# Stage two of a spectral block: the order of its sums, who negates and copies its output, and when the modulation columns are made

## The chip, the cores and the metric

One core of a Trainium2 chip. The metric is the device time of one execution in microseconds, the median of several runs. The profile is of one further execution, recorded by the hardware profiler.

## The reference

The block is a transformer layer with adaptive layer norms. `x` is 2048 x 512, all in float32:

```python
mod = (silu(c) @ w_mod).reshape(1, 6, 1, 512)
sa, ca, ga, sb, cb, gb = (mod[:, i] for i in range(6))
h = layernorm(x) * (1 + ca) + sa
y = irfft2(rfft2(h) * (w_r + 1j * w_i))     # over both axes, 2048 x 512
x = x + ga * y
h = layernorm(x) * (1 + cb) + sb
x = x + gb * (mish(h @ w1 + b1) @ w2)       # 512 -> 1376 -> 512
```

## The kernel before

The two-dimensional transform is done with matrix products. Stage one (to about 50 us) does the row transform of 512 and the first factor of the column transform, stage two (about 50 to 96 us) the second factor, the product with the spectral weights and the first factor back, stage three (about 96 to 142 us) the second factor back, the row transform back and `x + ga * y`. The rest is the MLP, in 8 blocks of 256 rows, in which TensorE works almost without a break.

The order of the work is written out by hand (`manual_schedule`), with no planner's costs or due times: the function's body is a list of calls, and the compute engines take their instructions in that order and wait where they have to. A load that waits for its buffer can be issued behind later ones: in the trace the last modulation load stands behind the first weight loads of stage three.

**Stage two** works on 17 groups of frequencies. Sixteen are ordinary (one of 3 and fifteen of 4 frequencies, 128 columns each), and the group of frequency zero has functions of its own (`z_in`, `z_mul`, `z_prod`, `z_back`, `z_out`). `seq` puts the zero group in position 4 of 0 to 16. For an ordinary group there are these steps:

- `p2_in`: TensorE transposes four tiles (L472), ACT copies them out of PSUM (L475), POOL adds the shift (`p2_shift`, L483).
- `p2_mul`: TensorE multiplies by a constant matrix (L492). The result lies in one of two banks "B" or in the bank `spare`, in turn.
- `p2_prod`: the complex product with the weights. ACT copies the two halves crosswise into `o` (L512, L513), POOL multiplies `o` by one part of the weights (L514), DVE multiplies the bank in place by the other (L515).
- `p2_add`: DVE adds both and writes the sum into `a_sb` (L521). This frees the bank of `p2_mul`.
- `p2_out` and `store_d`: TensorE multiplies by a constant matrix (L530) into one of two banks "D", and the result goes to `dd[0]` and `dd[1]`, 32 lanes each, as three planes: real part, imaginary part and the negated real part. ACT copies two planes for each of both halves (L387, 128x256), and the negated plane comes from POOL (L393, from the copy in SBUF), for the narrow groups from ACT (L391), and for the last group from DVE (L389, from PSUM).

The main loop runs over s = 1 to 19. Step s does the sum of position s, the product of position s + 1, the input of position s + 3 and the output of position s - 3. The first products are made ahead of it, in a loop over the first five inputs. Around these stand, by step:

- `mod_fetch` (SP's queue) and `mod_late` (DVE, L115): the modulation vectors `ga`, `sb`, `cb` and `gb`, 128 values at a time. Each of 16 columns is a load of 256 KB into one of four buffers and one DVE instruction that multiplies it by the spread-out silu(c) and sums it. `when` gives their steps, 3 to 18.
- `load_wq`: the weights of later groups (512 KB each, on ACT's queue, L558), into the place of the weights last used.
- `z_back` at step 5: the zero group's way back, with ACT and DVE copying from one bank and POOL writing zeros (L405 to L407, L453 to L456). Its target is `early[0]`, free after the first groups.
- `flat` and `spread`: the gate column goes out to DRAM and comes back spread over the partitions (ACT's queue); `mod_gate` (DVE, L552) then multiplies the constants `kiv` of the row transform back by `ga`.
- the loads of `kc` (two of 1 MB, ACT's queue, L604), the constants of stage three.

**Stage three** runs over 16 tiles: `p3_col(s)` (L675, L676: matmuls of `dd` with `kc`; ACT's copy L678), `p3_row(s - 1)` (L685: matmuls with `kiv`; DVE's L688 adds to `x`), statistics of the new `x` (`norm_sums`, DVE) and, every few tiles, `norm_scale` (ACT L127, L128 and four small DVE instructions). Beside them the MLP's weights are loaded on SP's queue (`load_w1`, `load_w2`) and split into two float32r parts (`split_w1`: ACT L629, POOL L630; `split_w2`, `sum_w2`: L726, L727, L723), and the first block's input is normalised and transposed. The second gate is spread there as well. The first tile needs every group's output in `dd[0]`.

## Time and profile before

| | before |
|---|---|
| median of 3 runs | 390.59 us (389.32 to 393.05) |
| profiled execution | 389.15 us |
| span in the profile (first to last instruction) | 387.1 us |
| granted TensorE clock | 0.998 |
| busy: PE, PE weight loads | 376.2 us (97%), 341.4 us (88%) |
| busy: DVE, ACT, POOL | 297.7 us (77%), 253.0 us (65%), 107.0 us (28%) |

The span leaves out 389.15 - 387.1 = 2.05 us around the first and the last instruction. PE is TensorE's matmuls, PEld its weight loads, DVE VectorE, ACT ScalarE, POOL GpSimd, SP the engine that only issues transfers here; ACTq and SPq are the queues of ACT and SP. L512 is line 512 of the kernel. Matmuls overlap and their ends are modelled, so a busy PE isn't always at its limit. In a timeline, brackets tell how long the engine was idle before an instruction and what ended that.

### The profile page before, as it was taken

To read this page: it belongs to the slowest core of one execution; us is meant where nothing else is said; L and a number is where in the kernel's file an instruction comes from. 1 tells how busy PE (TensorE), PEld (TensorE's weight loads), DVE (VectorE), ACT (ScalarE), POOL (GpSimd) and SP (SyncE) were. 2 spreads that over 40 slices of the span, in tenths; PEclk is the share of its full clock that TensorE was granted. 3 is DMA by queue.
4 is the path that set the end of the run, shared out by engine and by line. 5 is a ranking of instruction groups with operands and counts; after the bars stand their busy time and mean duration, and the time that the engine had idled before them with its cause. 6 is when DMAs were issued, how large, how long until landed. Compare 5 with 4: busy or idle time off the path is not lost.

```text
span 387.1 us, 7132 instructions
## 1 busy us (share of the span) xinstructions
PE 376.2 (97%) x2612; PEld 341.4 (88%) x2612; DVE 297.7 (77%) x674; ACT 253.0 (65%) x532; POOL 107.0 (28%) x149
## 2 busy tenths in 40 slices
PE   8999989897999999999999999999999999999996
PEld 8999857676999998999999998998999899899985
DVE  1898957788489989878757856965965885987994
ACT  1798787996459548965845755764674674594751
POOL 0587746899257713300000000000000010017000
PEclk9999999999999999999999999999999999999999
DMA  7999976898043411100100100100100200112011
GB/s 239 375 356 341 363 310 200 246 352 316 6 152 92 129 49 28 56 1 2 54 2 1 56 2 0 56 1 2 55 2 0 75 1 2 50 59 110 2 54 54
DMA packets 21747, 41.14 MB, mean 106 GB/s; under 512 B 4017, under 2 KB 7185, under 8 KB 21457
## 3 DMA queue, kind: packets, MB, share of 16 engines
q1 hardware_dynamic: 19552, 33.75, 25.3%
q10 hardware_dynamic: 2160, 6.95, 5.4%
q8 instruction: 20, 0.33, 0.4%
q14 instruction: 15, 0.11, 0.1%
HBM read 36.49 MB, written 4.20 MB: 105 GB/s over the span
## 4 chain that ended last, share of the span: by engine, by line
PE 80%; ACT 6%; issue 3%; POOL 3%; DVE 3%; DMA 3%; ACTq 0%; POOLq 0%; DVEq 0%
PE bank L817 24%; PE bank L764 20%; PE bank L766 10%; PE bank L208 4%; PE bank L253 3%; PE bank L809 2%; PE bank L685 2%; PE bank L830 2%; PE bank L654 2%; PE bank L675 2%; PE bank L676 2%; DMA wm<-in_w_mod_dram 1%; ACT buf L512 1%; DMA buf<-in_B_w_dram 1%; PE bank L264 1%
## 5 line engine op out<-in xcount | busy, mean ns | idle before, releaser
L774 ACT ACTIVATE buf<-bank,b1n 128x256 f32<-128x256 f32 (+1 forms) x88 | 40.8, 472 | 66.9 <-PE bank L766 66.5
L775 DVE TENSOR_TENSOR buf<-buf,bank 128x256 f32<-128x256 f32 (+1 forms) x88 | 35.4, 417 | 38.6 <-ACT buf L774 38.6
L746 POOL TENSOR_TENSOR buf<-buf,modr 128x512 f32<-128x512 f32 (+1 forms) x3 | 3.9, 1299 | 183.0 <-DVE al L727 148.3
L727 DVE TENSOR_TENSOR al<-buf,ah 128x512 fp32r<-128x512 f32 (+2 forms) x85 | 53.0, 647 | 0.9 <-ACT ah L726 0.9
L764 PE MATMUL bank<-h2e,w1h 128*128 128x512 f32 (+1 forms) x176 | 48.5, 397 | 0.0
L764 PE MATMUL bank<-h2o,w1h 128*128 128x512 f32 (+1 forms) x176 | 48.3, 396 | 0.0
L726 ACT CAST ah<-buf 128x512 fp32r<-128x512 f32 (+2 forms) x85 | 43.0, 549 | 1.4 <-DVE buf L791 1.1
L791 DVE TENSOR_TENSOR buf<-buf 128x128 f32<-128x128 f32 x148 | 40.8, 317 | 3.5 <-ACT buf L781 2.2
L781 ACT ACTIVATE buf<-buf 128x512 f32<-128x512 f32 (+1 forms) x48 | 28.6, 596 | 14.7 <-DVE buf L775 14.6
L817 PE MATMUL bank<-w2a,ah 128*128 128x256 f32 x161 | 34.9, 286 | 0.0
L764 PEld LDWEIGHTS bank<-h2e,w1h 128*128 128x128 f32 (+1 forms) x176 | 30.1, 187 | 4.5
L764 PEld LDWEIGHTS bank<-h2o,w1h 128*128 128x128 f32 (+1 forms) x176 | 30.1, 187 | 4.4
L817 PE MATMUL bank<-w2b,ah 128*128 128x256 f32 x147 | 31.8, 283 | 0.0
L766 PEld LDWEIGHTS bank<-h2e,w1l 128*128 128x128 f32 (+1 forms) x176 | 26.7, 185 | 4.2
L766 PEld LDWEIGHTS bank<-h2o,w1l 128*128 128x128 f32 (+1 forms) x176 | 26.7, 185 | 4.2
L766 PE MATMUL bank<-h2e,w1l 128*128 128x256 f32 (+1 forms) x176 | 27.8, 280 | 0.0
L766 PE MATMUL bank<-h2o,w1l 128*128 128x256 f32 (+1 forms) x176 | 27.8, 280 | 0.0
L817 PEld LDWEIGHTS bank<-w2a,ah 128*128 128x128 f32 x161 | 26.7, 191 | 0.0
L676 PE MATMUL bank<-kc,d 128*128 128x128 f32 x128 | 24.8, 276 | 0.7 <-POOL d L393 0.7
L675 PE MATMUL bank<-kc,d 128*128 128x128 f32 x128 | 24.9, 276 | 0.5 <-ACT d L387 0.5
L817 PEld LDWEIGHTS bank<-w2b,ah 128*128 128x128 f32 x147 | 24.6, 191 | 0.0
L122 DVE BATCH_NORM_STATS2 st<-x 128x6 f32<-128x512 f32 x32 | 22.0, 688 | 0.4
(219 smaller groups left out, 987.5 us busy)
## 6 DMA issues: line engine op xcount, KB each, us to landing
buf<-in_B_w_dram SPq DMA_DIRECT2D x20, 256.0 KB, 3.1
x<-in_A_x_dram SPq DMA_DIRECT2D x16, 256.0 KB, 4.8
xring<-in_x_t_dram SPq DMA_DIRECT2D x16, 256.0 KB, 4.7
wm<-in_w_mod_dram SPq DMA_DIRECT2D x16, 256.0 KB, 5.7
out_dram<-x SPq DMA_DIRECT2D x7, 512.0 KB, 2.6
mraw<-in_km_dram SPq DMA_DIRECT2D x16, 128.0 KB, 4.4
wqa<-in_w_q_dram SPq DMA_DIRECT2D x4, 512.0 KB, 7.1
wqb<-in_w_q_dram SPq DMA_DIRECT2D x4, 512.0 KB, 6.9
```

The source lines that it names most:

```text
L122: nc.vector.bn_stats(t, x[:, n, :])
L675: nc.tensor.matmul(o, dj[:, 0:128], kc[0][:, n, :], start=True, stop=False)
L676: nc.tensor.matmul(o, dj[:, 64:192], kc[1][:, n, :], start=False, stop=True)
L726: nc.scalar.copy(h, r)
L727: nc.vector.tensor_tensor(l, r, plain(h), op=ALU.subtract)
L764: nc.tensor.matmul(ps, w1h[:, k, fs], h[:, k], start=(k == 0), stop=False)
L766: nc.tensor.matmul(ps[:, 0:256], w1l[:, k, fs], h[:, k, 0], start=False, stop=(k == 3))
L774: nc.scalar.activation(o, ps[:, 256:], AF.Identity, bias=b1n[:rows, f:f + 1])
L775: nc.vector.tensor_tensor(o, o, ps[:, 0:256], op=ALU.add)
L781: nc.scalar.activation(o, o, AF.Mish)
L791: nc.vector.tensor_tensor(o, p, q, op=op)
L817: nc.tensor.matmul(o, a[p][:, e], w2[t][q][:, r], start=(own and half == 0 and t == 1 and i == 0), stop=(end and i == 2 and (n, half) != ( ...
```

## The change

- In the loop ahead of the main loop the sum of position 0 (`p2_add`) is written before the product of position 1 (`p2_prod`).
- `store_d` gets a kind. In an ordinary step ("busy") POOL negates the first half only and DVE the second, from PSUM. In steps without a modulation column, 9, 11 and 18, ("free") DVE copies the second half as well. The narrow groups ("all") and the last group ("last") are as before.
- The zeros for `z_back` are written at step 2, and its last ACT copy is moved ahead of DVE's copy.
- Modulation columns: 11 remain in stage two, at steps 3, 4, 5, 6, 8, 10, 12, 14, 15, 16 and 17. Five are made in stage three, two in its step 0 and one in each of steps 1 to 3; their loads go into the buffers "t", two from step 17 on, the others each after an earlier column.
- `load_wq` goes one step earlier, the second load of `kc` goes from step 13 to 12, `mod_gate` from step 15 to 13, and `plus_one` from stage two's step 16 to stage three's step 3.
- In stage three `flat` and `spread` of the second gate go from steps 2 and 4 to 5 and 7, and `norm_scale` of the first four tiles from steps 3 and 5 to 4 and 7.

```diff
-    def store_d(ps, q0, nq, other=None):
+    def store_d(ps, q0, nq, kind="all"):
...
             s = src[:, 32 * i:32 * i + 32]
-            nc.scalar.copy(dst[:, :, 0:2, q0:q0 + nq], s)
-            if other:
-                nc.vector.tensor_scalar(dst[:, :, 2, q0:q0 + nq], s[:, :, 0, :], -1.0, None, op0=ALU.mult)
-            elif nq < 4:
-                nc.scalar.mul(dst[:, :, 2, q0:q0 + nq], s[:, :, 0, :], -1.0)
+            to, minus = dst[:, :, 0:2, q0:q0 + nq], dst[:, :, 2, q0:q0 + nq]
+            if kind == "free" and i:
+                nc.vector.tensor_copy(to, s)
             else:
-                nc.gpsimd.tensor_scalar(dst[:, :, 2, q0:q0 + nq], dst[:, :, 0, q0:q0 + nq], -1.0, None, op0=ALU.mult)
+                nc.scalar.copy(to, s)
+            if kind == "all":
+                nc.scalar.mul(minus, s[:, :, 0, :], -1.0)
+            elif kind == "last" or i:
+                nc.vector.tensor_scalar(minus, s[:, :, 0, :], -1.0, None, op0=ALU.mult)
+            else:
+                nc.gpsimd.tensor_scalar(minus, dst[:, :, 0, q0:q0 + nq], -1.0, None, op0=ALU.mult)
...
+    def z_space():
+        return early[0][:, 0, 0:256], early[0][:, 0, 256:512]
...
         turned(t1, pc[:, 0:P])
-        nc.gpsimd.memset(t2[0:96, 0:P], 0.0)
         nc.scalar.copy(t2[0:32, 0:P], pc[0:32, P:2 * P])
+        nc.scalar.copy(t2[64:96, 0:1], pc[64:96, P:P + 1])
         nc.vector.tensor_copy(t2[32:64, 1:P], pc[32:64, 2 * P - 1:P:-1])
-        nc.scalar.copy(t2[64:96, 0:1], pc[64:96, P:P + 1])
...
-        store_d(pd, q0, nq, g == seq[-1])
+        store_d(pd, q0, nq, "all" if nq < 4 else "last" if g == seq[-1] else "free" if free else "busy")
...
-    when = (3, 4, 5, 6, 7, 8, 9, 10, 11, 12, 13, 14, 15, 16, 17, 18)
+    when = (3, 4, 5, 6, 8, 10, 12, 14, 15, 16, 17)
...
+    def mod_second(k):
+        w = buf("t")
+        nc.sync.dma_start(w, wm_d[5 - (k == 0), (k - 1) % 4])
+        return w
...
                 p2_mul(seq[i // 2 - 1])
-                p2_prod(seq[i // 2 - 1])
                 if i == 4:
                     p2_add(seq[0])
+                p2_prod(seq[i // 2 - 1])
...
-            if 3 <= s < len(seq) + 3 and seq[s - 3] and groups[seq[s - 3]][0] < 32:
-                load_wq(groups[seq[s - 3]][0] // 4 + 8)
+            if 2 <= s < len(seq) + 2 and seq[s - 2] and groups[seq[s - 2]][0] < 32:
+                load_wq(groups[seq[s - 2]][0] // 4 + 8)
...
+            if s == 2:
+                nc.gpsimd.memset(z_space()[1][0:96, 0:P], 0.0)
+            if s == len(seq):
+                second = [mod_second(k) for k in range(2)]
...
-                p2_out(seq[s - 3])
+                p2_out(seq[s - 3], s != 13 and not work_mod[s])
...
-            if s == 15:
+            if s == 13:
                 mod_gate()
-            if s == 16:
-                plus_one(cols[:, 1, 1, :], cols[:, 1, 1, :])
-            if s in (11, 13):
+            if s in (11, 12):
...
+        for k in ((0, 1), (2,), (3,), (4,))[s] if s < 4 else ():
+            mod_column(second[k], gcol[:, 1, k - 1:k] if k else cols[:, 1, 1, 3:4], 1.0, second[k], scp)
+            if k < 3:
+                second.append(mod_second(k + 2))
+        if s == 3:
+            plus_one(cols[:, 1, 1, :], cols[:, 1, 1, :])
-        if s == 2:
+        if s == 5:
             st["gb"] = flat("gb", gcol[:, 1])
-        if s == 4:
+        if s == 7:
             spread(gbr, st["gb"])
...
-        if s in (3, 5):
-            norm_scale(s - 3, s - 1)
+        if s in (4, 7):
+            norm_scale(*((0, 2) if s == 4 else (2, 4)))
```

More of the change, by code (lines that the diff above doesn't have):

```diff
@@ L450, in z_back @@
         nc.tensor.transpose(pc[0:96, P:2 * P], y[:, 160:256], ident)
-        t1, t2 = early[0][:, 0, 0:256], early[0][:, 0, 256:512]
+        t1, t2 = z_space()
         turned(t1, pc[:, 0:P])
-        nc.gpsimd.memset(t2[0:96, 0:P], 0.0)
         nc.scalar.copy(t2[0:32, 0:P], pc[0:32, P:2 * P])
+        nc.scalar.copy(t2[64:96, 0:1], pc[64:96, P:P + 1])
         nc.vector.tensor_copy(t2[32:64, 1:P], pc[32:64, 2 * P - 1:P:-1])
-        nc.scalar.copy(t2[64:96, 0:1], pc[64:96, P:P + 1])
         st["t", 0] = t1, t2
@@ L521, in p2_add, with p2_out @@
             nc.vector.tensor_tensor(slot(g), st.pop(("pb", g))[:, 0:w], st.pop(("o", g)), op=ALU.add)
-    def p2_out(g):
+    def p2_out(g, free):
         if g == 0:
```

## The prediction

> **What bounds the kernel now.** First the busy time of each engine in stretches of 5 us (columns: stretch, length, busy us and instruction count of PE, PEld, DVE, ACT, POOL, then the granted clock, DMA share, GB/s), because the page's mean hides the stages.
>
> ```profile
> 75.00:80.00 5.00, 5.00 (x34) 3.83 (x32) 4.16 (x10) 4.85 (x12) 5.00 (x10) 1.00 0.90 250
> 100.00:105.00 5.00, 5.00 (x47) 5.00 (x46) 3.04 (x6) 2.50 (x5) 1.05 (x1) 1.00 0.02 0
> 115.00:120.00 5.00, 4.46 (x39) 4.06 (x38) 4.38 (x7) 4.97 (x10) 3.55 (x5) 1.00 0.26 59
> 120.00:125.00 5.00, 5.00 (x48) 5.00 (x46) 4.82 (x7) 4.62 (x12) 3.75 (x4) 1.00 0.33 89
> ```
>
> In stage two (50 to 96 us) ACT and POOL are full and DVE is at 4.2 of 5; from 100 us on PE and its weight loads are full, with one hole near 115 us. So a change in stage two can only bring the start of stage three forward, by what ACT and POOL lose. The timeline of one step (step 12; start, duration, line; in brackets the idle time ahead) shows how tight it is:
>
> ```profile
> 82.16 0.59 ACT L512 ACTIVATE buf<-bank 64x512 f32<-64x512 f32 x1
> 82.77 0.58 ACT L513 COPY buf<-bank 64x512 f32<-64x512 f32 x1
> 83.37 0.59 ACT L475 COPY buf<-bank 128x512 f32<-128x512 f32 x1
> 83.38 0.70 DVE L515 TENSOR_TENSOR bank<-bank,wqb 128x512 f32<-128x512 f32 x1 [0.27 <-ACT buf L513]
> 83.47 1.29 POOL L514 TENSOR_TENSOR buf<-buf,wqb 128x512 f32<-128x512 f32 x1
> 83.85 0.65 ACT L387 COPY d<-bank 128x256 f32<-128x256 f32 x2
> 83.99 0.68 DVE L115 SCALAR_TENSOR_TENSOR wm<-wm,bank 128x512 f32<-128x512 f32 x1
> 84.53 0.59 ACT L512 ACTIVATE buf<-bank 64x512 f32<-64x512 f32 x1
> 84.72 0.21 POOL L483 TENSOR_TENSOR buf<-buf,saz 128x4 f32<-128x4 f32 x1
> 84.80 0.69 DVE L521 TENSOR_TENSOR a_sb<-bank,buf 128x512 f32<-128x512 f32 x1
> 84.87 1.03 POOL L393 TENSOR_SCALAR d<-d 128x128 f32<-128x128 f32 x2
> 85.14 0.58 ACT L513 COPY buf<-bank 64x512 f32<-64x512 f32 x1
> ```
>
> ACT's five instructions follow each other without a gap, 84.53 - 82.16 = 2.37 us a step. POOL needs 1.29 + 0.21 + 1.03 = 2.53, less overlaps about 2.4. DVE needs about 0.61 + 0.68 + 0.69 = 2.0. **ACT sets the step, POOL a hair behind.**
>
> **Part by part.** I write T for the end of the second copy (L513) of position 14 in the order of groups: 85.14 + 0.58 = 85.72 before.
>
> *First sum ahead of the second product.*
>
> ```profile
> 53.57 1.00 POOL L514 TENSOR_TENSOR buf<-buf,wqa 128x384 f32<-128x384 f32 x1 [0.83 <-ACT buf L513]
> 54.30 0.29 DVE L406 COPY early<-bank 128x127 f32<-128x127 f32 x1 [0.21 <-ACT early L405]
> 56.12 0.55 DVE L521 TENSOR_TENSOR a_sb<-bank,buf 128x384 f32<-128x384 f32 x1
> 56.82 1.10 PE L492 MATMUL bank<-early,kf 128*128 128x512 f32 x2 [1.63 <-DVE a_sb L521]
> 57.95 0.59 ACT L512 ACTIVATE buf<-bank 64x512 f32<-64x512 f32 x1 [0.65 <-PE bank L492]
> 60.60 0.32 ACT L387 COPY d<-bank 128x192 f32<-128x192 f32 x1 [0.36 <-PE bank L530]
> ```
>
> PE waits for the first sum, since the product of position 3 needs its bank. The sum's POOL input is ready at 53.57 + 1.00 = 54.57 and DVE is free at 54.59, so it can run there and not at 56.12: PE starts 1.5 us earlier, ACT's 0.65 vanishes, and of the 0.36 some 0.2 (PE's other inputs come from ACT itself). Gain 0.85; between 0.6 (only the first wait, if the second product's DVE half is pushed back) and 1.0 (both).
>
> *Zeros early, copies in another order.*
>
> ```profile
> 65.84 0.28 DVE L406 COPY early<-bank 128x127 f32<-128x127 f32 x1
> 66.36 0.20 POOL L453 MEMSET early<- 96x128 f32 x1
> 66.59 0.26 ACT L454 COPY early<-bank 32x128 f32<-32x128 f32 x1 [1.28 <-POOL early L453]
> 66.87 0.28 DVE L455 COPY early<-bank 32x127 f32<-32x127 f32 x1 [0.75 <-ACT early L454]
> 67.19 0.15 ACT L456 COPY early<-bank 32x1 f32<-32x1 f32 x1 [0.35 <-DVE early L455]
> ```
>
> ACT idles 1.28 + 0.35 = 1.63. The memset sits behind POOL's products; at step 2 it has POOL's gap of that step and costs nothing (0.2 without it). But the rows also show ACT and DVE taking turns at one bank: L455 waits for L454 and L456 for L455, though they read different partitions. So L454 still waits for DVE's L406, which ends at 66.12 by its row. I keep 66.12 less what DVE gains: 66.59 - 66.12 = 0.47, and the 0.35 in full, less the new negation that step 4 puts into DVE's queue ahead of L406 (0.25). About 0.65. Ends: 0.3 (DVE late) and 1.63 (the whole idle time).
>
> *Negations and copies shared.* In the ordinary step POOL keeps one negation (1.03/2 = 0.52) and DVE gets the other. Its price is L389's row (in the tail, below): 0.29, some 0.25 from start to start. It reads the bank that ACT copies and, as the last of those rows shows (0.44 of idle time for L387), waits for that copy; L521 and L515 are queued behind it. In the step above the second L387 ends near 84.50, DVE is free at 84.67: nothing waits, and DVE's 2.0 becomes 2.25, below 2.37. So POOL's relief and DVE's burden both lie beside ACT, worth nothing.
> In the steps with no mod column (9, 11 and 18; 13 is excepted) the second copy goes to DVE too. A 128x256 copy there isn't in the trace: L406 (128x127) took 0.29, L521 (128x512, two inputs) 0.69; between them 0.42, which I take, ends 0.29 and 0.69. DVE then has 0.61 + 0.42 + 0.25 + 0.69 = 2.0, ACT 2.37 - 0.32 = 2.05, POOL 1.29 + 0.21 + 0.52 = 2.0. Steps 9 and 11 gain 0.3 each: 0.6 in all (0 if the turn-taking on the bank makes DVE late, 0.65 at most). Step 18 is in the tail.
>
> The 8 weight loads (L558) go one step earlier on ACT's queue. Their slots' readers (L514, L515) are two steps old by then, and they are only issued by ACT: 0. The second half of kc (1 MB) goes one step earlier: it is behind the gate row's spread in the queue and before stage three needs it: 0.
>
> So T comes 0.85 + 0.65 + 0.6 = **2.1 us earlier**.
>
> *The tail.* From T on, no inputs are left and DVE decides:
>
> ```profile
> 91.36 1.36 DVE L552 TENSOR_TENSOR kiv<-kiv,modr 128x512 f32<-128x512 f32 x1
> 93.47 1.13 PE L530 MATMUL bank<-kv,a_sb 128*128 128x128 f32 x8 [0.73 <-ACT d L387]
> 95.26 0.69 DVE L115 SCALAR_TENSOR_TENSOR wm<-wm,bank 128x512 f32<-128x512 f32 x1 [0.72 <-DMA wm<-in_w_mod_dram]
> 95.87 0.29 DVE L389 TENSOR_SCALAR d<-bank 128x128 f32<-128x128 f32 x1
> 96.26 0.46 PE L676 MATMUL bank<-kc,d 128*128 128x128 f32 x2 [0.70 <-POOL d L393]
> 96.60 0.29 DVE L389 TENSOR_SCALAR d<-bank 128x128 f32<-128x128 f32 x1 [0.44 <-ACT d L387]
> ```
>
> Stage three's chain of matmuls starts at 96.26 = T + 10.54 before (its named POOL releaser is long done by then; it is L389's end at 96.16). The change takes out two mod columns (0.68 each) and the wait for the last one's DMA (0.72), and puts in five negations (0.25), a copy (0.42) and its negation. The gate multiply (L552, 1.36) moves ahead of the last products.
> In DVE's order from T, by start-to-start times: L515 0.61; wait for ACT's copy, negation: 1.42; gate 2.70; L521 3.3; L515 3.9; mod 4.6; negation 4.85; L521 5.45; L515 6.05; mod 6.75; negation 7.0; L521 7.6; mod 8.3; negation 8.55; mod 9.2; negation 9.5. PE's output of step 18 needs the bank that the negation of step 16 frees (8.55): 9.65. Then ACT's copy 10.07, DVE's 10.5. PE's last output runs 9.65 to 10.7, ACT's copy of it to 11.12, the negation to 11.44, PE starts at T + 11.5. That is **0.95 later** than T + 10.54. [...]
> L552 has both inputs in SBUF and took 1.36 where L521 of the same size took 0.69, beside a busy POOL; in step 13 POOL is as busy.
> [...]
>
> *Mods moved into stage three.* Five mod columns (0.68 each, 3.4 in sum) go to DVE in its steps 0 to 3, with five loads of 256 KB on SP's queue ahead of weight loads.
>
> ```profile
> 100.78 0.69 DVE L688 TENSOR_TENSOR x<-x,bank 128x512 f32<-128x512 f32 x1 [3.89 <-PE bank L685]
> 103.45 0.69 DVE L688 TENSOR_TENSOR x<-x,bank 128x512 f32<-128x512 f32 x1 [1.05 <-PE bank L685]
> 112.22 0.30 ACT L127 ACTIVATE rstd<-mv,eps 128x2 f32<-128x2 f32 x1 [1.03 <-DVE mv L123]
> 113.66 0.62 ACT L629 CAST w1h<-buf 128x512 fp32r<-128x512 f32 x1 [0.91 <-DMA buf<-in_B_w_dram]
> 142.46 0.69 DVE L688 TENSOR_TENSOR x<-x,bank 128x512 f32<-128x512 f32 x1 [0.66 <-PE bank L685]
> buf<-in_B_w_dram SPq DMA_DIRECT2D x20, 256.0 KB, 3.1
> wm<-in_w_mod_dram SPq DMA_DIRECT2D x16, 256.0 KB, 5.7
> ```
>
> DVE idles 3.89 + 1.05 there. The first two loads wait for nothing late. The third waits for the first column's buffer: after the tail's last copy and negation (12.2 by the count above) the column ends at T + 12.9, 1.4 after stage three's start. At 3.1 us for a load (5.7 is from the full stretch) the third column ends at 1.4 + 3.1 + 0.7 = 5.2, where the first L688 is due at 100.78 - 96.26 = 4.5; the fourth and fifth add up to the third L688 being some 0.8 later than before. PE bears that: the bank it needs is two rows old (2 x 2.67, by the two L688 rows). DVE regains it at the end, where it had 0.66 to spare. Cost 0, ends 0 and 2.5 (rival 2).
>
> *Statistics and gate spread moved.* Near 112 to 116 us ACT waits 1.03 for statistics and 0.91 for a weight load, and PE loses 5.00 - 4.46 = 0.54 in that stretch. The statistics wait goes (step 7 instead of 5), and the gate spread's 256 KB no longer travel beside that load. Gain 0.54 (0 if the hole moves to step 7).
>
> **Sum.** 2.1 - 0.95 + 0.54 = 1.7 us. The profiled execution took 389.15 (span 387.1, 2.05 around it): 387.45 after. The median shown is 1.44 above it, so I give 390.59 - 1.7 = **388.9**.
>
> **Rivals.**
> 1. *The tail is not lost* (0.18): the gate multiply of step 13 fits into DVE's slack of steps 13 and 14 and the chain is shorter by 1.3. For it: two columns and a DMA wait less. Against: DVE's row of instructions above has no slack. Gain 3.0, 387.6; with the zeros at their upper end 386.6.
> 2. *Slower: DVE starves in stage three* (0.12). With loads of 5.7 us, not 3.1, the fifth column waits for two of them in a row: 1.4 + 2 x 5.7 + 2 x 0.7 = 14.2 after stage three's start, and the third L688 with it, where it ran at about 10.3 before: 3.9 later. DVE has 0.62 and 0.18 of idle time in the two stretches from 115 us and 0.66 at the end to regain it, 1.5 in all, so the first MLP block starts some 2.5 us later. It decides, against the 1.7, from loads of about 5.3 us. Against: the DMA share there was 0.02, and only weight loads join. 390.59 - 1.7 + 2.5 = 391.4.
> 3. *Nothing moves* (0.18): ACT's waits turn into others (L406 for L454, the output matmuls for L387) and the tail eats the rest. 390.6.
>
> **Chances and range.** Forecast 0.52, rivals 0.18, 0.12, 0.18. A measurement of this kernel can't tell under 1% (3.9 us) from no change: its three runs spread over 3.7 us. Over 1% faster needs the best ends of most terms (0.85 or 1.0, 1.63, 0.65, and no loss in the tail): 0.15. Over 1% slower needs more than rival 2: 0.07. The rest, 0.78, is within 1%. The range runs from the better ends of rival 1, 385.6, to a little above rival 2, 391.8.
>
> **What would show it.** PE's matmul of position 3 near 55.2, ACT's L512 of that position without idle time; L454 waiting for DVE, not POOL; steps of 2.37 us, 2.05 in steps 9 and 11; POOL with idle time in every step; L513 of position 14 ending near 83.6; DVE without idle time from there to stage three's first L676 near 95.1; no hole of PE near 115. Wrong would be above all: DVE setting the step in the ordinary steps (over 2.4 us), or stage three's first rows waiting for a mod column's DMA.

## The result and the profile after

The changed kernel takes 386.7 us (median of 5 runs, 385.79 to 387.25) beside 389.82 us of the kernel before (5 runs): a ratio of 0.9898, 95% interval 0.9855 to 0.9941. Its profiled execution took 387.25 us (span 385.5), the one before 389.15 (span 387.1). All runs below list their mean granted TensorE clock, which turns out to matter.

Three stretches of the changed kernel, in the view of busy time by stretch that the prediction began with (columns as there):

```profile
75.00:80.00 5.00, 5.00 (x34) 3.85 (x33) 4.40 (x10) 4.88 (x11) 4.37 (x7) 1.00 0.88 265
115.00:120.00 5.00, 5.00 (x47) 5.00 (x47) 4.60 (x8) 4.25 (x11) 4.35 (x7) 1.00 0.62 157
125.00:130.00 5.00, 4.30 (x39) 4.13 (x38) 4.79 (x10) 2.21 (x5) 2.45 (x3) 1.00 0.66 201
```

POOL went from 5.00 to 4.37 of 5 in stage two and ACT stayed full, as foreseen. The hole near 115 us is gone (PE 5.00 instead of 4.46), but PE now loses 0.70 between 125 and 130.

The timeline of the changed kernel, in the order of the prediction's steps. Line numbers have moved: the sum is L527, the crosswise copies L518 and L519, POOL's product L520, the output matmuls L536, ACT's copy and negation L391 and L393, DVE's copy L389, the negations of DVE and POOL L395 and L397, the zero group's copies L460 to L462, the gate multiply L563, stage three's two kinds of matmul L688 and L689.

```profile
54.41 0.56 DVE L527 TENSOR_TENSOR a_sb<-bank,buf 128x384 f32<-128x384 f32 x1
55.12 1.10 PE L498 MATMUL bank<-early,kf 128*128 128x512 f32 x2
57.12 0.59 ACT L518 ACTIVATE buf<-bank 64x512 f32<-64x512 f32 x1
59.62 0.32 ACT L391 COPY d<-bank 128x192 f32<-128x192 f32 x1 [0.22 <-PE bank L536]
...
65.36 0.25 ACT L460 COPY early<-bank 32x128 f32<-32x128 f32 x1 [1.04 <-DVE early L410]
...
71.11 0.59 ACT L518 ACTIVATE buf<-bank 64x512 f32<-64x512 f32 x1
73.48 0.59 ACT L518 ACTIVATE buf<-bank 64x512 f32<-64x512 f32 x1
75.57 0.59 ACT L518 ACTIVATE buf<-bank 64x512 f32<-64x512 f32 x1
75.58 0.42 DVE L389 COPY d<-bank 128x256 f32<-128x256 f32 x1 [0.18 <-ACT d L391]
...
83.01 0.58 ACT L519 COPY buf<-bank 64x512 f32<-64x512 f32 x1
84.99 1.08 DVE L563 TENSOR_TENSOR kiv<-kiv,modr 128x512 f32<-128x512 f32 x1
85.06 1.41 POOL L397 TENSOR_SCALAR d<-d 128x128 f32<-128x128 f32 x1
87.18 0.68 DVE L115 SCALAR_TENSOR_TENSOR wm<-wm,bank 128x512 f32<-128x512 f32 x1
87.78 0.29 DVE L395 TENSOR_SCALAR d<-bank 128x128 f32<-128x128 f32 x1
88.13 1.16 PE L536 MATMUL bank<-kv,a_sb 128*128 128x128 f32 x8 [0.95 <-DVE d L395]
90.13 1.16 PE L536 MATMUL bank<-kv,a_sb 128*128 128x128 f32 x8 [0.84 <-DVE d L395]
94.05 0.49 PE L688 MATMUL bank<-kc,d 128*128 128x128 f32 x2 [0.46 <-ACT d L391]
94.66 0.46 PE L689 MATMUL bank<-kc,d 128*128 128x128 f32 x2
...
105.48 0.68 DVE L701 TENSOR_TENSOR x<-x,bank 128x512 f32<-128x512 f32 x1
...
123.86 1.51 POOL L643 TENSOR_TENSOR w1l<-buf,w1h 128x512 fp32r<-128x512 f32 x1 [3.25 <-ACT w1h L642]
124.75 0.64 DVE L135 SCALAR_TENSOR_TENSOR ve<-mv,rstd 128x4 f32<-128x4 f32 x1
125.42 0.16 DVE L135 SCALAR_TENSOR_TENSOR ve<-ve,rstd 128x4 f32<-128x4 f32 x1
125.68 0.94 POOL L643 TENSOR_TENSOR w1l<-buf,w1h 128x352 fp32r<-128x352 f32 x1 [0.30 <-ACT w1h L642]
125.82 0.82 DVE L147 SCALAR_TENSOR_TENSOR nmr<-mv,rstd 128x4 f32<-128x4 f32 x1
...
129.31 1.13 PE L698 MATMUL bank<-kiv,buf 128*128 128x128 f32 x8 [0.70 <-ACT w2hi L739]
```

What to see: position 3's matmul starts at 55.12 and ACT no longer waits for it. L460 waits for DVE, not POOL. A step is 73.48 - 71.11 = 2.37 us with two ACT copies and 75.57 - 73.48 = 2.09 where DVE makes one. T, the end of the second copy of position 14, is 83.01 + 0.58 = 83.59 (85.72 before). In the tail, PE's output matmuls wait for DVE's negations: the one at 88.13 starts when L395 at 87.78 is done, and L395 stood behind a column.

Stage one's length varies between executions (its end from 48.28 to 50.81 us over the traces), so I measure from the start of L279, stage two's first matmul (49.04 here, 49.23 before): T, then **P**, the start of stage three's first matmul of the second kind (94.66; before L676 at 96.26), and **S**, from there to the last add to `x` (before L688 at 142.46: 46.20). After that add all traces have the same length, 244.60 to 244.70. The table gives all runs; the last column counts the timed runs with a mean clock of 0.996 or less.

| kernel | median us (runs) | ratio to before, 95% | T | P | S | low clock |
|---|---|---|---|---|---|---|
| before | 389.82 (5) | | 36.49 | 47.03 | 46.20 | 32 of 76 later ones |
| before_again | 390.62 (1) | | 36.49 | 47.41 | 47.70 | 1 of 1 |
| after | 386.7 (5) | 0.9855 to 0.9941 | 34.55 | 45.62 | 46.14 | 0 of 5 |
| after_again | 386.61 (6) | 0.9881 to 0.9949 | 34.59 | 45.67 | 45.20 | 1 of 6 |
| late_sum | 387.71 (9) | 0.9911 to 0.9962 | 35.28 | 46.35 | 45.19 | 2 of 9 |
| late_zeros | 387.59 (12) | 0.9894 to 0.995 | 34.91 | 45.98 | 45.28 | 1 of 12 |
| no_free | 387.23 (12) | 0.9891 to 0.9944 | 35.13 | 46.16 | 45.20 | 1 of 12 |
| pool_negates | 386.75 (6) | 0.9872 to 0.9937 | 35.14 | 45.52 | 45.25 | 0 of 6 |
| gate_19 | 386.34 (6) | 0.9848 to 0.9932 | 34.56 | 45.04 | 45.94 | 0 of 6 |
| act_tail | 385.3 (6) | 0.9844 to 0.9904 | 34.58 | 44.46 | 45.13 | 0 of 6 |
| mods_back | 387.85 (12) | 0.9896 to 0.9955 | 35.13 | 46.00 | 45.42 | 3 of 12 |
| mods_alone | 388.12 (12) | 0.9942 to 0.9992 | 36.49 | 46.88 | 45.22 | 2 of 12 |
| tail_gap | 391.01 (10) | 1.0012 to 1.0067 | 34.57 | 48.45 | 47.24 | 9 of 10 |
| best | 384.27 (6) | 0.9801 to 0.9886 | 34.55 | 43.29 | 46.06 | 0 of 6 |

The two traces of the changed kernel (after, after_again) agree to 0.05 in T and P, so these marks tell apart what the medians can't. The two traces of before agree in T, but their P differs by 0.38, for a reason told below. S is 45.1 to 45.4 where PE has no hole in stage three and 45.9 to 46.2 where it has one; the two larger values belong to traces in which the clock fell.

### The profile page after: what moved, and what is told of

Its sections match the earlier page's. It is cut to its first block, busy times and chain, and to the rows that moved or that the text cites. A ratio compares the mean times of both kernels' runs of the same rounds, so it can differ in the third digit from the quotient of the medians.

```text
span 385.5 us, 7140 instructions
## 1 busy us (share of the span) xinstructions
PE 375.8 (97%) x2612; PEld 341.3 (89%) x2612; DVE 300.9 (78%) x691; ACT 251.9 (65%) x529; POOL 99.6 (26%) x135
## 3 DMA queue, kind: packets, MB, share of 16 engines
HBM read 36.49 MB, written 4.20 MB: 106 GB/s over the span
## 4 chain that ended last, share of the span: by engine, by line
PE 82%; DVE 6%; ACT 6%; issue 3%; POOL 1%; DMA 1%; ACTq 0%; DVEq 0%; POOLq 0%
PE bank L830 24%; PE bank L777 20%; PE bank L779 10%; PE bank L208 4%; PE bank L698 3%; PE bank L253 3%; PE bank L688 3%; PE bank L689 3%; PE bank L822 2%; PE bank L843 2%; PE bank L667 2%; ACT buf L519 1%; PE bank L264 1%; PE bank L255 1%; PE bank L254 1%
## 5 line engine op out<-in xcount | busy, mean ns | idle before, releaser
L739 ACT CAST ah<-buf 128x512 fp32r<-128x512 f32 (+2 forms) x85 | 43.0, 548 | 1.4 <-DVE buf L804 1.1
L688 PE MATMUL bank<-kc,d 128*128 128x128 f32 x128 | 24.9, 276 | 0.5 <-ACT d L391 0.5
L689 PE MATMUL bank<-kc,d 128*128 128x128 f32 x128 | 24.8, 276 | 0.1
```

The lines of the kernel that those rows point to most:

```text
L688: nc.tensor.matmul(o, dj[:, 0:128], kc[0][:, n, :], start=True, stop=False)
L689: nc.tensor.matmul(o, dj[:, 64:192], kc[1][:, n, :], start=False, stop=True)
L739: nc.scalar.copy(h, r)
```

## The experiments

**after_again**: the changed kernel once more, beside its variants.

> The changed kernel unaltered, as the mark for the others on the same chip, and a second trace of it. Theory A (the sum of the prediction, by terms): stage three's first L689 again within 0.3 us of 94.66 in its trace, time 386.0 to 387.3. Theory B (what the timed runs gained beyond the 1.9 us of the two profiled executions, 3.1 against 1.9, comes from stalls in stage three that differ from run to run): start of stage three the same, but the end of the last L701 moves by 0.5 to 1.5 us between two traces.

386.61 us. T and P came back. S was 0.94 shorter, as Theory B has it, and the hole of 0.70 at 129.31 is missing: whether it is there differs between executions of one kernel.

**late_sum** writes the first sum behind the second product again:

```diff
-                if i == 4:
-                    p2_add(seq[0])
                 p2_prod(seq[i // 2 - 1])
+                if i == 4:
+                    p2_add(seq[0])
```

> Undoes one part: the product of position 1 is written ahead of the sum of position 0 again. Theory A: the product matmul of position 3 waits for the sum again (1.6 us of PE idle), the end of L519 of position 14 and stage three's start come 0.6 to 0.85 us later than in the unaltered kernel, time +0.7. Rival (the slack of later steps swallows it, since POOL's chain in steps 3 to 6 is late anyway): both marks within 0.2 us, time +0.0.

Its timeline has the three waits of before, unchanged:

```profile
57.33 1.10 PE L498 MATMUL bank<-early,kf 128*128 128x512 f32 x2 [1.63 <-DVE a_sb L527]
58.46 0.59 ACT L518 ACTIVATE buf<-bank 64x512 f32<-64x512 f32 x1 [0.65 <-PE bank L498]
61.11 0.32 ACT L391 COPY d<-bank 128x192 f32<-128x192 f32 x1 [0.36 <-PE bank L536]
```

T and P are 0.7 later than in the changed kernel. So the order of the first sum is worth 0.7, all of it from this chain.

**late_zeros** writes the zeros in `z_back` again and restores the order of its copies:

```diff
+        nc.gpsimd.memset(t2[0:96, 0:P], 0.0)
         nc.scalar.copy(t2[0:32, 0:P], pc[0:32, P:2 * P])
-        nc.scalar.copy(t2[64:96, 0:1], pc[64:96, P:P + 1])
         nc.vector.tensor_copy(t2[32:64, 1:P], pc[32:64, 2 * P - 1:P:-1])
+        nc.scalar.copy(t2[64:96, 0:1], pc[64:96, P:P + 1])
...
-                nc.gpsimd.memset(z_space()[1][0:96, 0:P], 0.0)
```

> Undoes one part: POOL writes the zeros inside step 5 again and the third copy stands behind DVE's. Theory A: L460 waits for POOL again and L461's successor for DVE, position 14 and stage three come 0.4 to 0.7 us later, time +0.5. Rival (with one negation less POOL reaches the zeros in time): only the order of the copies counts, 0.2 to 0.35 us.

T is 0.34 later (34.91 against 34.55 and 34.59). Its timeline shows which half of the edit this is:

```profile
65.07 0.20 POOL L460 MEMSET early<- 96x128 f32 x1
65.41 0.25 ACT L461 COPY early<-bank 32x128 f32<-32x128 f32 x1 [1.05 <-DVE early L410]
...
66.02 0.15 ACT L463 COPY early<-bank 32x1 f32<-32x1 f32 x1 [0.35 <-DVE early L462]
```

The memset, though late in the program, ends at 65.27 and delays nobody: POOL has time now that DVE makes half of the negations, and ACT waits for DVE's copy with and without the edit (1.05 and 1.04). Only the 0.35 of the changed order came out, as the rival has it.

**no_free** lets ACT make both copies in steps 9, 11 and 18 too; DVE keeps the second negation:

```diff
-                p2_out(seq[s - 3], s != 13 and not work_mod[s])
+                p2_out(seq[s - 3], False)
```

> Undoes one part: in steps 9, 11 and 18 ACT makes the second copy again; DVE's and POOL's negations stay. Theory A: position 14 comes 0.55 to 0.65 us later (two steps of 2.37 in place of 2.05), the tail is up to 0.2 us shorter, time +0.5. Rival (POOL or DVE limits those steps anyway): 0.0 to 0.2 later.

T 0.56 later, P 0.5: the free copies are worth what the two short steps show, 2 x (2.37 - 2.09) = 0.56.

**pool_negates** takes all of DVE's share back (ACT copies both halves, POOL negates both):

```diff
-            if kind == "free" and i:
-                nc.vector.tensor_copy(to, s)
-            else:
-                nc.scalar.copy(to, s)
+            nc.scalar.copy(to, s)
...
-            elif kind == "last" or i:
+            elif kind == "last":
```

> Undoes the sharing alone: ACT copies both halves in every step and POOL negates both, all else as in the changed kernel. Theory A (DVE's queue sets the tail, and its negations with their waits for ACT are what makes it long): L519 of position 14 ends 0.6 to 0.9 us later (no 2.05 us steps, POOL late at step 5), but stage three starts 7.7 to 8.5 us after that and not 11.07, so 1.8 to 2.4 us earlier than in the unaltered kernel; time about 384.7. Rival (the sharing is worth what it relieves POOL and ACT of, the tail is set by the mod columns and the gate multiply): stage three starts 0.6 to 1.0 us later, time about 387.5.

Beside no_free, only the place of the second negation differs. T is the same (35.14 and 35.13), so in ordinary steps it is indeed free on DVE. P is 0.64 earlier with POOL: in the tail the negation is dearer on DVE. Against the changed kernel, the sharing as a whole gains 0.56 at T and has lost it at P (45.52 against 45.62 and 45.67). Neither theory came: A has P 1.8 to 2.4 earlier, the rival 0.6 to 1.0 later. What held it is in the timeline of this kernel, where the gate multiply is L560, POOL's shift L486 and its negation L394:

```profile
84.58 1.27 POOL L517 TENSOR_TENSOR buf<-buf,wqb 128x512 f32<-128x512 f32 x1
85.09 1.69 DVE L560 TENSOR_TENSOR kiv<-kiv,modr 128x512 f32<-128x512 f32 x1
85.82 1.04 POOL L486 TENSOR_TENSOR buf<-buf,saz 128x4 f32<-128x4 f32 x1
...
94.25 0.53 POOL L394 TENSOR_SCALAR d<-d 128x128 f32<-128x128 f32 x1
```

DVE and POOL were both slower where they overlapped: the multiply took 1.69 where it began inside POOL's product (1.08 in the changed kernel), and POOL's shift behind that product took 1.04 instead of 0.20. From there POOL works on without a break to the end of the tail, where it makes eight negations in a row. The last row, from a view of just these tenths, is the seventh of them, of position 15 into `dd[0]`. It ends at 94.25 + 0.53 = 94.78, and PE's first matmul of the second kind, which needs it, starts at 94.83. So here POOL's queue is the end of the tail.

**gate_19** moves the gate multiply to the end of step 19, behind DVE's last negation:

```diff
-            if s == 13:
+            if s == 19:
                 mod_gate()
```

> Moves one part: the gate multiply (L563, 1.1 to 1.4 us beside a busy POOL) goes from step 13 to the end of step 19, behind DVE's last negation. Theory A, as I now read the row of DVE in the trace: from position 14 to the last sum DVE also waits for ACT's L519, so taking 1.0 us out of its row brings the last sum forward by 0.4 us and stage three with it, 45.3 us after the first matmul of the shift sum in place of 45.7; the multiply takes about 0.69 there, since POOL rests, and delays nothing; time -0.4. Rival, the price that the prediction put on the multiply: it costs the tail its whole length, start 44.4 to 44.7, time -1.0 to -1.3.

P is 0.6 earlier than in the changed kernel: about half of its 1.08 us was on the path at step 13, between the two expectations. There it took 1.08 too, and not the 0.69 expected. The median, 386.34, lies within the spread.

**act_tail** gives copies and negations of all groups from position 11 on to ACT:

```diff
-        ... "all" if nq < 4 else "last" if ...
+        ... "all" if nq < 4 or q0 >= groups[seq[11]][0] else "last" if ...
```

> A version that may beat both: the changed kernel, but from step 14 on (position 11) ACT copies and negates both halves, as it does for the narrow groups, since it is idle 3.2 of 5 us from 90 us on. Theory A: L519 of position 16 ends some 0.5 us later (two more negations of 0.27 on ACT in step 14), DVE's row from there has no negation, the last sum ends near 90 and stage three starts at 92.2 to 92.8 and not 94.66; if stage three stays as long, 384.6. Rival (POOL's last product or the mod columns hold the last sum as late as now): start at 94.2 or later, time within 0.5 us of the unaltered kernel.

P is 1.2 earlier (44.46), between the two expectations; the median is 385.3. PE's wait in the tail is now for ACT. This fits a ring of output matmuls, copies and negations through two banks "D", in which whoever has the negation sets the tail:

```profile
89.08 2.05 PE L536 MATMUL bank<-kv,a_sb 128*128 128x128 f32 x16 [1.08 <-ACT d L393]
```

**mods_back** puts all 16 columns, the second gate's way out and back and the statistics back in their old places, with the rest of the change kept (with columns in steps 9, 11 and 18 there are no free copies, as in no_free):

```diff
-    when = (3, 4, 5, 6, 8, 10, 12, 14, 15, 16, 17)
+    when = (3, 4, 5, 6, 7, 8, 9, 10, 11, 12, 13, 14, 15, 16, 17, 18)
...
-        if s in (4, 7):
-            norm_scale(*((0, 2) if s == 4 else (2, 4)))
+        if s in (3, 5):
+            norm_scale(s - 3, s - 1)
```

> Undoes one part: all 16 modulation columns in stage two again, at steps 3 to 18, with the second gate's way and the statistics of stage three at their old steps; sharing of the negations, zeros, first sum and the gate multiply at step 13 as in the changed kernel. Since every step then has a column, no step gives its second copy to DVE. From the shift sum's first matmul the unaltered kernel's marks are 34.6 us (end of L519 of position 14) and 45.7 us (first L689). Theory A: 35.2 for the first, since the two short steps are gone; 47.7 to 48.4 for the second, since DVE's row gets two more columns of 0.68 and the wait of about 0.7 for the last load back; stage three itself 0 to 0.5 us shorter, its DVE being relieved of five columns; time 1.5 to 2.5 us above the unaltered kernel. Rival (the columns only change places, DVE pays for them in stage three what it saves in stage two): start of stage three 2 us later, but its end at most 0.7 us later, time +0.5.

I expected the five columns to come back into the tail; in this trace they did not. Against no_free P is 0.16 earlier, not later. Here S was 45.42 with the old statistics and no hole, so the old places don't force the hole of before. The median is 0.6 above that of no_free all the same (387.85 and 387.23; without the runs of low clock 387.66 and 387.03). One trace of each doesn't show where that goes.

**before_again** is a further profile of the kernel before, whose median lay above its first profiled execution.

> The kernel before unaltered, for a second trace. Its timed runs spread from 387.9 to 393.5 us with a median of 390.5, those of the changed kernel from 385.8 to 388.5, and the one trace of before is of a run of 389.15, below its median. Theory B (a good part of the 3.1 to 3.9 us between the medians is a loss in stage three of before that its first trace shows only in part): stage one ends within 1 us of 49.2 and stage three starts 47.0 us after it as in the first trace, but stage three takes more than the 46.2 us of that trace where the run is slower. Theory A (the sum of the prediction holds, 1.7 us): 47.0 and 45.4 to 46.2, and a slow run is slow by its stage one. Theory C (the wait for the last modulation load, 0.72 us in the first trace, grows in slow runs): the start of stage three comes later than 47.0.

The first fence is the first profile of before by stretch, the second the new one, the third the new one's timeline:

```profile
92.75:96.16 3.41, 1.62 (x10) 1.26 (x10) 2.69 (x8) 1.02 (x3) 3.41 (x8) 1.00 0.60 220
96.00:98.00 2.00, 1.74 (x15) 1.77 (x16) 0.45 (x2) 0.37 (x1) 0.60 (x2) 1.00 0.04 8
98.00:100.00 2.00, 2.00 (x20) 2.00 (x19) 0.00 (x0) 0.70 (x2) 0.00 (x0) 1.00 0.00 0
```

```profile
92.62:96.03 3.41, 1.62 (x10) 1.26 (x10) 2.30 (x8) 0.91 (x3) 3.41 (x8) 1.00 0.60 220
96.00:98.00 2.00, 1.63 (x8) 1.66 (x8) 0.56 (x4) 0.37 (x1) 0.31 (x1) 0.51 0.04 8
98.00:100.00 2.00, 2.00 (x13) 2.00 (x13) 0.00 (x0) 0.33 (x1) 0.00 (x0) 0.64 0.00 0
```

```profile
94.78 0.49 PE L675 MATMUL bank<-kc,d 128*128 128x128 f32 x2 [0.46 <-ACT d L387]
95.37 0.69 DVE L115 SCALAR_TENSOR_TENSOR wm<-wm,bank 128x512 f32<-128x512 f32 x1 [1.11 <-DMA wm<-in_w_mod_dram]
95.98 0.29 DVE L389 TENSOR_SCALAR d<-bank 128x128 f32<-128x128 f32 x1
96.37 0.77 PE L676 MATMUL bank<-kc,d 128*128 128x128 f32 x2 [1.10 <-POOL d L393]
```

The signs of Theories B and C both came, P later and S longer, but neither has the reason. The last column waited 1.11 us for its load (0.72 in the first profile), the negation behind it was late, PE stood for 1.10 us (0.70), and **then the granted clock fell**: 0.51 and 0.64 in the next two stretches of 2 us, where the first profile shows 1.00. PE ran 8 and 13 matmuls there instead of 15 and 20. S grew by 1.50, P by 0.38. The timed runs of before have the trace of it too: 32 of 76 have a mean clock of 0.996 or less, with a median of 391.45 us; the other 44 a median of 389.32. Of the 68 runs of the changed kernel and those variants that keep the columns in stage three (without tail_gap, and mods_alone told below), 5 have it. Two experiments test this. The first row of each of the first two fences is taken up after them.

**mods_alone** is the kernel before with only the five columns moved and what that forces in stage three:

```diff
-    when = (3, 4, 5, 6, 7, 8, 9, 10, 11, 12, 13, 14, 15, 16, 17, 18)
+    when = (3, 4, 5, 6, 8, 10, 12, 14, 15, 16, 17)
...
+        for k in ((0, 1), (2,), (3,), (4,))[s] if s < 4 else ():
+            mod_column(second[k], ...)
...
-        if s in (3, 5):
-            norm_scale(s - 3, s - 1)
+        if s in (4, 7):
+            norm_scale(*((0, 2) if s == 4 else (2, 4)))
```

> Before, with only the moved modulation columns (and what they force in stage three: plus_one, the second gate's way out and back and norm_scale in the later steps). First sum, zeros, copies and negations as before. The last column in stage two and the wait of 0.72 to 1.11 us for its load go from in front of the last negations. Clock theory: that wait holds TensorE back by 0.70 us in one trace of before and 1.10 in the other, and where the gap is long the granted clock falls for some 3 us behind it (0.51 and 0.64 in the two stretches of 2 us from 96 us in the second trace), 1.5 us lost; half of before's executions have a mean clock of 0.996 or less and a median of 391.4, the others 1.0 and 389.4. Without the wait nearly all executions show a mean clock of 0.998 or more, stage three's first matmul of the second kind comes 0.6 after the first of the first kind (0.6 to 1.0 earlier than before), and the median is 388.4 to 389.0. Prediction's pricing (moved columns worth nothing): 390.2 to 390.7, and the low mean clock as often as before. Rival, wait without clock: 389.7 to 390.0, the low clock as often as before, being chance of the execution.

388.12 us, ratio 0.9967. Two of 12 runs have the low clock; the runs of the kernel before beside them had it in 5 of 23 only (27 of 53 beside the other experiments), so these runs alone don't settle how often. Among the other runs the medians are 387.99 and 389.26: 1.3 faster without any clock in it. Beside the first trace of before, its trace puts 0.98 of that into S (45.22, no hole) and 0.15 into P, where 0.6 to 1.0 was expected. The rows show why P gained so little:

```profile
95.03 0.28 DVE L389 TENSOR_SCALAR d<-bank 128x128 f32<-128x128 f32 x1
95.53 0.53 POOL L393 TENSOR_SCALAR d<-d 128x128 f32<-128x128 f32 x1
96.11 0.49 PE L681 MATMUL bank<-kc,d 128*128 128x128 f32 x2 [0.59 <-POOL d L393]
```

DVE's negation for `dd[0]` is done at 95.31, but POOL has eight negations in a row here, to 96.55. The second row, from a view of just these tenths, is the seventh, of position 15 into `dd[0]`. It ends at 95.53 + 0.53 = 96.06, and PE starts at 96.11. In the first trace of before the same negation of POOL ran at nearly the same time and ended just ahead of DVE's (96.16):

```profile
95.57 0.53 POOL L393 TENSOR_SCALAR d<-d 128x128 f32<-128x128 f32 x1
```

So with the wait on DVE gone, POOL's queue held P. (Around the change of stage DVE's row doesn't keep strictly to the written order: two columns of stage three, written behind the last group's two negations, run ahead of them and between them, at 94.42 and 96.05 in mods_alone, where the negations start at 95.03 and 96.66.)

**tail_gap** makes the opposite test: the changed kernel with the first of the last group's negations made eight times, which computes the same and only makes PE stand.

```diff
-                nc.vector.tensor_scalar(minus, s[:, :, 0, :], -1.0, None, op0=ALU.mult)
+                for _ in range(8 if kind == "last" and not i else 1):
+                    nc.vector.tensor_scalar(minus, s[:, :, 0, :], -1.0, None, op0=ALU.mult)
```

> After, with the first of the last group's two negations made eight times instead of once: 7 more DVE instructions, 0.20 us from start to start, 1.4 us in front of stage three's first matmul of the second kind, so that TensorE has a gap of about 1.4 us there. Clock theory: in most executions the granted clock falls behind the gap for some 3 us, the mean clock is 0.996, and the time is 386.7 + 1.4 + 1.5 = 389.6; in executions where it doesn't fall, 388.1. Rival (the clock's fall has nothing to do with the gap): 388.0 to 388.3 in all, with a mean clock of 0.999 or 1.0 as for the changed kernel.

The gap came out at twice the size: the repeated negations follow each other every 0.32 us (1.26 for four) and not every 0.20, and a column stands between them. Its view by stretch and its timeline:

```profile
94.39:97.80 3.41, 0.71 (x6) 0.74 (x7) 2.72 (x10) 0.37 (x1) 0.00 (x0) 1.00 0.85 259
96.00:98.00 2.00, 0.91 (x7) 0.94 (x8) 1.18 (x5) 0.37 (x1) 0.00 (x0) 0.95 0.98 313
98.00:100.00 2.00, 2.00 (x12) 2.00 (x11) 0.00 (x0) 0.20 (x1) 0.00 (x0) 0.50 0.61 222
100.00:102.00 2.00, 2.00 (x14) 2.00 (x14) 0.00 (x0) 0.39 (x1) 0.00 (x0) 0.70 0.00 0
```

```profile
93.90 1.26 DVE L396 TENSOR_SCALAR d<-bank 128x128 f32<-128x128 f32 x4
97.09 0.46 PE L690 MATMUL bank<-kc,d 128*128 128x128 f32 x2 [2.93 <-issue]
```

Nine of 10 runs show a mean clock of 0.986 to 0.995, with a median of 391.17 us; the tenth shows 1.0 and 389.35. P is 2.8 later than in the changed kernel (48.45), and 386.6 + 2.8 = 389.4 is just the run without the fall. The fall costs 1.8 more. So a gap of PE in front of stage three brings the clock down, which is now shown by making one; that the gap of 0.7 to 1.1 us in before does it in under half of the executions rests on one trace with, one without, and the clocks of the timed runs.

In both traces the fall lasts 3.41 us. In stretches of 0.5 us the clock of before_again is 0.53 from 96.00, 0.56 from 99.00 and 0.50 between them, so half from 96.03 to 99.44; that of tail_gap is 0.80 from 97.50, 0.79 from 101.00 and 0.50 between them, so half from 97.80 to 101.21. In the 3.41 us ahead of them PE was busy for 1.62 us in before_again and 0.71 in tail_gap, and for 1.67 ahead of the fall at the very end of the first trace of before, at 385.63. But that trace has 1.62 in a stretch of this length up to 96.16 too, and the clock stayed at 1.00 behind it. So what decides whether a gap like that of before brings the clock down is not shown.

The runs of the other kernels: in pool_negates, gate_19, act_tail and best no stretch of this length in the tail, wherever it is laid, has PE busy for under 0.62 of it, and none of their 24 runs has the low clock; in the traces of after, after_again, late_sum, late_zeros, no_free and mods_back there are some of 0.46 or 0.47 (1.61 us in after, up to 90.16), and 8 of 56 runs have it. The least of before is no lower, 1.62 of 3.41 us in both traces, and 32 of its 76 runs have the low clock. So whether its load often comes later still, or something else adds to it, stays open.

**best** combines what the above points to: gate multiply at step 19, the outputs of positions 13 and 15 in the banks "A" that are free by then, copies and negations of positions 11, 12, 15 and 16 on ACT, and the negations of 13 and 14 on POOL.

```diff
-            elif kind == "last" or i:
+            elif i and kind != "pool":
...
-        pd = bank("D")
+        at = seq.index(g)
+        pd = bank("A" if at in (13, 15) else "D")
...
+        ... "all" if nq < 4 or at in (11, 12, 15, 16) else "pool" if at > 12 else ...
...
-            if s == 13:
+            if s == 19:
                 mod_gate()
```

> A version that may beat both, from what the runs so far show: the changed kernel with the gate multiply at the end of step 19, the outputs of steps 16 and 18 in the bank pair A, which has no use there any more, so that TensorE needn't wait for two banks D, and from step 14 on no negation on DVE: ACT copies and negates in steps 14, 15, 18 and 19, in steps 16 and 17 ACT copies and POOL negates. Theory A (two banks D and DVE's negations make the tail): last sum 40.4 us after the first matmul of the shift sum, its output's matmuls at once behind it, stage three 43.2 to 43.8 us after it, where the changed kernel has 45.6 and the version with ACT's negations 44.5; time 384.3 to 384.8. Rival (ACT's copies in a row are the bound): 44.3 or more, time within 0.4 of the version with ACT's negations, 385.3.

384.27 us, ratio 0.9843 (0.9801 to 0.9886): 1.6% less than before, and below the changed kernel's 386.7, beside which it wasn't timed directly. P is 43.29, 2.3 earlier than after the change. Its profiled execution, with a stage one that ended at 50.81 and a hole of 0.70 at 128.67, took 386.6; the median is 2.3 below it.

## Why the prediction was right, and where not

The measured 386.7 lies in the range of 385.6 to 391.8 and the time moved the way forecast, but it is 2.2 below the forecast of 388.9. Part by part:

**First sum: right in kind, 0.7 for 0.85.** Position 3's matmul started at 55.12 (forecast 55.2), ACT's 0.65 went, and 0.22 of the 0.36 stayed where 0.16 was forecast.

**Zeros: 0.34 for 0.65.** The turn-taking that the rows showed was read rightly: L460 waits for DVE and the 0.35 came out in full. The term that failed is the other one, the 0.47 that ACT should gain by the early memset. It counted on DVE's copy staying put in the step; that copy is still behind a column and ACT still idles 1.04 for it. The working also adds up wrongly: 0.47 + 0.35 - 0.25 is 0.57, not 0.65.

**Free copies: 0.56 for 0.6.** The interpolated copy took 0.42, exactly the value taken between 0.29 and 0.69, which for a guess between two rows is luck. **Negations on DVE in ordinary steps: 0**, as forecast. Together T came 36.49 - 34.55 = 1.94 earlier for 2.1.

**The tail: 0.53 lost for 0.95.** From T to P it was 10.54 before, and 94.66 - 83.59 = 11.07 after, not 11.5. The mechanism stands: PE's outputs wait 0.95 and 0.84 for negations that are late in DVE's row. Mis-sized were the gate multiply, which took 1.08 and not 1.36, and the moved columns: the count saw them as part of a row without slack, but mods_back and mods_alone both put their effect on P at 0.16 or less, with opposite signs. One reading was wrong: POOL's negation was not "long done" when stage three started before. It ended at 96.10, 0.06 ahead of DVE's, so taking work from DVE alone could hardly bring P forward (mods_alone), and in the tail POOL's relief was not worth nothing. What remains between the undone parts and the whole stays open: 0.7 for the sum, 0.34 for the zeros and a loss of 0.1 for the sharing make 0.9, P gained 1.4. The rest may be the gate multiply's earlier step, the earlier loads, or parts that need each other, as DVE's relief needs POOL's; these weren't run alone.

**Stage three: 0 to 1.0 for 0.54.** The hole near 115 (0.54 in the first trace of before, 0.57 in the second) is in no trace with the moved statistics. It isn't in mods_back with the old ones either, so that the statistics made it is not shown. In mods_alone S is 0.98 shorter than in the first trace of before, more than the hole alone. But three of the ten traces with the moved columns and without the made gap (after, gate_19, best) have another hole of 0.5 to 0.7 near 129. "0 if the hole moves" was the right lower end, "0.54" was the hole without what follows it. What decides whether that one opens was not found: the releaser that the profile names for it, ACT's L739, is only inferred, and S is the one mark in which two executions of the same kernel differ by as much as the whole term.

**The step that failed most** is the last: 390.59 - 1.7. The prediction set its own execution, 389.15, 1.44 below the median of three runs and carried that 1.44 over as if it belonged to both kernels. Without it the forecast would have been 387.45, which is 0.75 above the measured median and not 2.2. Little of it came back in the changed kernel, whose own profile, 387.25, even lies above its median. In before it goes with the clock. The clocks of those three runs aren't on record, but three of the four later sets of before have medians of 390.25 to 390.61 and a low clock in 27 of 53 runs, the fourth 389.48 and 5 of 23. With executions at full clock alone the change is 389.32 - 386.6 = 2.7 us, where the sum gives 1.7; by the marks P and S of the traces it is 1.5 (after) or 2.4 (after_again), the difference being S, 46.14 with the hole near 129 and 45.20 without. The rows for it were on the page: the wait of 0.72 for the last column's load and PE's 0.70, both of which the prediction shows. The wait was counted as one more term of the tail; what a longer wait would do to PE, and PE's pause to the clock, wasn't asked. The 0.998 of the first profile of before is no sign of such a fall: it comes from the last 1.5 us of the span, when PE has no matmul left (0.50 from 385.63 us on).

Of the rivals, the first (387.6, "the tail is not lost") had about the right time for the wrong reason: the tail was lost. The second didn't come. The third add to `x` runs 105.48 - 94.66 = 10.8 after P, where it ran 10.3 after it before: 0.5 later, not 3.9 (the forecast itself had 0.8). The loads of the moved columns, in the changed kernel's list of DMA issues (count, size of one, median us to landing), were as short as the forecast took them:

```profile
buf<-in_w_mod_dram SPq DMA_DIRECT2D x5, 256.0 KB, 2.9
```

The third, that everything is eaten, was the fate of one part, the sharing: 0.56 won at T and lost at P.

## What to carry to other kernels

Compare the profiled execution with the timed runs, clock by clock, before subtracting anything: behind a median 1.4 us above the profile there was here a second thing, a fall of the clock in four of ten executions. A stall of the matrix engine just ahead of a dense stage may cost twice, once for the wait and once for the clock after it (2.8 and 1.8 us in tail_gap), so a late load in front of such a stage is worth moving even where its own wait looks small. Two queues can end a stage within 0.1 us of each other (96.10 and 96.16 here), and relieving one of them alone then brings next to nothing (0.15 in mods_alone). And in a tail through two buffers look for the engine that frees the buffer: work taken from a full engine and given to that one is won in the steady steps and lost at the end (0.56 us at T here, nothing left of it at P).

## What the runs showed of the hardware

- The granted clock fell to 0.50 for 3.41 us about a pause of PE: in before_again, with a pause of 1.10 us, from 96.03 (PE starts again at 96.37); in tail_gap, with 2.93 us, only after the matmuls had started again at 97.09 (1.00 from 97.00 to 97.50, 0.80 from there to 98.00). It was back at 1.00 while PE was busy without a break. In the first trace of before, with a pause of 0.70 us, it stayed at 1.00. PE's share of the 3.41 us ahead doesn't tell these apart (1.62 us in both traces of before, told behind tail_gap).
- The gate multiply, with both inputs in SBUF, took 1.08 in after, where it began 0.07 ahead of POOL's negation, in best, where POOL worked during its first 0.17 only (to 93.34, the multiply from 93.17), and in gate_19; 1.36 in the tail before and 1.69 in pool_negates, where it began 0.40 and 0.76 ahead of the end of a POOL product. Beside it POOL's negation took 1.41 in after (0.53 otherwise) and its shift 1.04 in pool_negates (0.20). Beside a negation of DVE, which reads PSUM, POOL's stayed at 0.53 (after: POOL's at 87.67, DVE's at 87.78). DVE's steps on 128x4 values: L135 takes 0.16 at 125.42, but 0.64, and L147 0.82, where they start inside POOL's L643, and both end as that does (124.75 + 0.64 = 125.39 beside 125.37, 126.64 beside 126.62). The rows give the times and not what causes them.
- The same DVE negation repeated into the same place took 1.26 for four in tail_gap, 0.32 each, where another instruction follows a negation after 0.20 (91.63 to 91.84 there is 0.21, 93.10 to 93.30 0.20).
